# A gated linear recurrence followed by a SiLU block: 32x32 transposes of k and q that write their blocks side by side

## The chip, the cores and the metric

The kernel runs on one core of one Trainium2 chip. The metric is the device time of one execution in microseconds (us). Before the change the median of three runs is 561.26 us (560.49, 561.26 and 562.18).

## The reference

Two blocks follow each other. The first is a recurrence over 768 tokens for each of 4 batches and 8 heads of 48 dimensions; the second takes its output, laid out as 3072 tokens of 384 values, through two matrices with SiLU between them. All data are float32 on the chip.

```python
for t in range(S):                       # q, k, v, alpha: (4, 8, 768, 48)
    state = alpha[:, :, t, :, None] * state + np.einsum('bhd,bhe->bhde', k[:, :, t], v[:, :, t])
    y[:, :, t] = np.einsum('bhd,bhde->bhe', q[:, :, t], state)
x = y.transpose(0, 2, 1, 3).reshape(3072, 384)
h = x @ w_in                             # (384, 2048)
g = h * (1.0 / (1.0 + np.exp(-h)))
out = g @ w_out                          # (2048, 384)
```

## The kernel before

The recurrence is cut into 24 chunks of 128 tokens: 6 stretches of time for each of 4 batches (`NT = 24`; chunk n has stretch `n // 4` and batch `n % 4`). Within a chunk the products of alpha are taken by scans, so that the recurrence becomes ordinary matrix products: `kp` is k times a product of the alphas that follow, `p` (also called `qp`) is q times a product of the alphas up to it divided by a common factor, and the scores are `kp` against `qp`, masked so that no token sees a later one. A state of 48x48 for each head carries from chunk to chunk.

Heads are handled in pairs: in the tiles that the scans use, partition 64u + d holds dimension d of the heads with number 2g + u, and the free axis holds the four pairs g with 128 tokens each. The inputs come from memory with tokens, not dimensions, across the partitions, so they have to be transposed. The first 8 chunks (`n < NA`) do this on TensorE. The other 16 do it on VectorE, 32x32 elements at a time, and these are what the change is about.

For these 16 chunks `load` (L466) brings in `at`, `kt` and `qt` (alpha, k and q, four DMAs each). A partition holds four consecutive tokens of each head pair: token 4b + j lies in row b of a block of 32 rows, at place j, with its 48 dimensions side by side. `turned` (L694) transposes all of this in one VectorE instruction: for each pair g and each j it takes 32 rows by 32 dimensions and turns them into 32 dimensions by 32 values of b. These 32 values belong to tokens j, 4 + j, 8 + j and so on, so before the change they are written with a step of four elements, which puts the 128 tokens of a pair into their natural order.

Three tiles are made this way in each chunk:

- `al` from `at`, in `products` (L698). A scan over it (L722) gives `u`, and later another one (L752, in `quotient`) gives `p`. The scans need the tokens in order.
- `turn` from `kt`, in `products` (L730). It is multiplied by `u` into `kp`: L737 for the first two head pairs, L739 for the other two, whose halves of 64 tokens are written in exchanged order.
- `turn` from `qt`, in `quotient` (L742, transposed at L756). It is multiplied by `p` in place (L758).

After a transpose the tile that it has read is free, and the next chunk's load into it is issued at once. `turn` is one buffer, used in turn by the k tile, the q tile and `flip` (L760), which transposes `kp` once more (L768) and sends it through memory to turn it over for the state update.

Around this runs the SiLU block for tokens that are already through the recurrence. `enter` (L917) multiplies by `w_in` with a scheme that saves products at the price of sums on VectorE (L944, and sums of inputs and of weights at L582 to L587); `leave` (L1021) multiplies by `w_out` in a like manner (L1033, L1042, L1074 to L1085). Their pieces are dealt out over the steps by a plan of due times (`fill`, L1166), four slots a step. A step of a late chunk holds the scores of the chunk before, then `products` and `quotient` of its own, then the values and states of the chunk before. `audit` (L657) checks the inputs' magnitudes by reading them once more and reducing them on VectorE (L685).

TensorE's instructions of this part, the copies and scalings marked so, and VectorE's sums of inputs and of weights keep the order in which the program gives them; the others may be moved within their engine by a scheduler that goes by its own estimates of cost. All loads are issued from SP's queue, the stores up to the last group from GpSimd's.

Of the kernel before, what the change touches and what calls it, by code (L numbers as in the profile page):

```python
# [13 lines left out]
ALU = mybir.AluOpType  # L14
# [341 lines left out]
def quotients(  # L356
# [20 lines left out]
    dve, act, gps = nc.vector, nc.scalar, nc.gpsimd  # L377
# [25 lines left out]
    CH = C // 2  # L403
# [28 lines left out]
    def out_bank(i, n):  # L432
        return outs[i].tile([128, 512], F32, name="ps_o")[:, 0:n]

    def ps_attn(n=C):
        return ps_a.tile([128, 512], F32, name="ps_a").rearrange("p (j c) -> p j c", c=n)
# [29 lines left out]
    def load(n, names="akq"):  # L466
        if n == NT:
            return
        c = ctxs.setdefault(n, dict(zip(("ci", "b"), divmod(n, B))))
        b, rows = c["b"], slice(c["ci"] * C, c["ci"] * C + C)  # L470
        for name, src in (("a", alpha), ("k", k), ("q", q)):
            if name not in names:
                continue
            x = src[b, :, rows, :]
            if n < NA:
                c[name] = nat[name][n % NIN]
                nc.sync.dma_start(c[name][:, :, 0:D], x.transpose([1, 0, 2]))
                continue

            c[name] = late["quads"][name]
            for u in range(2):
                for i in range(2):
                    r = 64 * u + 32 * i
                    nc.sync.dma_start(
                        c[name][r : r + 32, 32 * (1 - i) :][:, 0 : 4 * NP * D].rearrange(
                            "p (g c) -> p g c", g=NP),
                        x[u::2].rearrange("h (b j) d -> b h (j d)", j=4))
# [48 lines left out]
    def turns(x, n):  # L538

        return x[(n + 1) % 2]  # L540
# [149 lines left out]
    def tokens(t):  # L690

        return t[:, 1 : NP * W + 1].rearrange("p (j c) -> p j c", c=W)[:, :, 0:C]

    def turned(x, to):  # L694
        x = x[:, 32:].rearrange("p (g j d) -> p g j d", j=4, d=D)
        dve.transpose(to.rearrange("p g (b j) -> p g j b", j=4), x[:, :, :, 0:32])

    def products(n):  # L698

        c = ctxs[n]  # L700
        sg = seg[0 if late else n % 2]
        ps = {}

        for name in ("a", "k", "q"):
            if n >= NA:
                if name == "a":
                    turned(c[name], tokens(sg))
                    load(n + 1, "a")
                continue
            if n < GB and name != "a":  # L710

                at = "kq".index(name)
                ps[name] = (bank(at) if n == 1 else out_bank(at, 512)).rearrange("p (j c) -> p j c", c=C)
            else:
                ps[name] = ps_attn()
            for j in range(NP):
                pe.transpose(ps[name][:, j, :], c[name][:, 2 * j : 2 * j + 2, :], ident)
            if name == "a":
                act.copy(tokens(sg), ps[name])  # L719
        end = NP * W  # L720
        u = upool.tile([128, end + 1], F32, name="u")
        dve.tensor_tensor_scan(u[:, end - 1 :: -1], sg[:, end:0:-1], one[:, end:0:-1],  # L722
                               0.0, ALU.mult, ALU.add)

        dve.tensor_single_scalar(least[:, n, :], u[:, 0:end:W], 2.0**-64, ALU.max)
        kp = c["kp"] = turns(kps, n) if n < NA else kps[0]
        ut = tokens(u)
        if n >= NA:
            ps["k"] = late["turn"].tile([128, NP, C], F32, name="turn")
            turned(c["k"], ps["k"])  # L730
            load(n + 1, "k")
        if n < NA:
            dve.tensor_tensor(kp, ps["k"], ut, ALU.mult)
            quotient(n, sg, ps["q"])
            return
        j = NP // 2
        dve.tensor_tensor(kp[:, 0:j], ps["k"][:, 0:j], ut[:, 0:j], ALU.mult)  # L737
        k, ut = [x[:, j:].rearrange("p j (e c) -> p j e c", e=2) for x in (ps["k"], ut)]
        dve.tensor_tensor(kp[:, j:].rearrange("p j (e c) -> p j e c", e=2)[:, :, ::-1], k, ut, ALU.mult)  # L739
        c["sg"] = sg  # L740

    def quotient(n, sg=None, q=None):  # L742

        c = ctxs[n]
        if sg is None:
            if n < NA:
                return
            sg = c.pop("sg")
        end, iv = NP * W, inv
        dve.reciprocal(iv[:, 0:end:W], least[:, n, :])  # L750
        p = turns(qps if n < NA else [qps[0], late["p"]], n)
        dve.tensor_tensor_scan(p[:, 0:end], sg[:, 0:end], iv[:, 0:end], 0.0, ALU.mult, ALU.add)  # L752
        qp = c["qp"] = tokens(p)
        if q is None:
            q = late["turn"].tile([128, NP, C], F32, name="turn")
            turned(c["q"], q)  # L756
            load(n + 1, "q")
        dve.tensor_tensor(qp, q, qp, ALU.mult)  # L758

    def flip(n):  # L760
# [133 lines left out]
    def bank(i, n=512):  # L894
        return banks[turn[i]].tile([128, 512], F32, name="ps_m")[:, 0:n]
# [289 lines left out]
    for step in range(STEPS):  # L1185
        if step == 1:
            load(NIN)
        stages = [[(scores, 1)], [(products, 0)], [(values, 1)], [(states, 1)]]
        if step == 1:

            stages = stages[1::-1] + stages[2:]
        elif step >= NA:
            stages = [[(land, 1), (scores, 1)], [(products, 0)], [(quotient, 0)],
                      [(values, 1), (states, 1), (flip, 0)]]
        for slot, group in enumerate(stages):
            for stage, lag in group:
                n = step - lag
                if not 0 <= n < NT:
                    continue
                stage(n)  # L1200
                if stage is values:
                    bridged = n + 1
                if stage is states and n + 1 + NIN < NA:
                    load(n + 1 + NIN)
                if stage is states and n + NV < NT:
                    load_v(n + NV)
            if step * SLOTS + slot == (NA + 1) * SLOTS - 1:
                x = decayed.rearrange("p (o i c) -> p o i c", o=2, c=C)
                for r, o in later:
                    gps.memset(x[r, o, :, 0:CH], 0.0)  # L1210
            fill(step, slot)
            if step * SLOTS + slot >= NA * SLOTS - 1 and conv_done[1] == NFT and not late:
                settle()
# [12 lines left out]
    for i, (x, op, bound, holds) in enumerate(checks):  # L1226
        e = ends[:, i : i + 1]
# [6 lines left out]
    ps = ps_attn()[0:1, 0, 0:1]  # L1234
# [64 lines left out]
```

## Time and profile before

The profiled execution has a span of 558.1 us; the median of the runs is 561.26 us, 3.2 us more, which lies around the span.

| what | value |
|---|---|
| span of the profiled execution | 558.1 us |
| median of three runs | 561.26 us |
| granted TensorE clock, mean of the core | 0.994 |
| L696 `al` transposes | 16 of 1134 ns |
| L722 scan to `u`, L752 scan to `p` | 24 of 1249 ns, 24 of 1246 ns |
| L944 products' sums from PSUM | 56 of 684 ns |
| L1033 sums | 72 of 708 ns |
| DMA, mean rate | 126 GB/s |

In the views that follow, PE is TensorE, PEld its loading of weights, DVE VectorE, ACT ScalarE and POOL GpSimd. A row of groups gives line, engine, operation, what is written and read, the shapes, the number of instructions, then after the bar their busy time in us and the mean of one in ns, and after the second bar the engine's idle time just before them with what ended it. A row of the timeline gives start and length in us, and in brackets the idle time before it and the instruction that ended that wait. A row of waits gives who waited for whom: us in total, how many times, and the longest. An instruction of VectorE that depends on the one before it starts after that one's end; one that doesn't can start a little before it.

### The profile page before, as it was taken

How to read it: one execution, taken by the hardware profiler on the slowest of the kernel's cores; microseconds unless marked ns; L12 is line 12 of the kernel's file. 1: busy time of each engine (PE TensorE's matmuls, PEld its weight loads, DVE VectorE, ACT ScalarE, POOL GpSimd, SP SyncE). 2: the span in 40 equal slices, each digit the busy share in tenths (PEclk: the TensorE clock that was granted, in tenths of full speed). 3: DMA queues.
4: the chain of work that ended last, by engine and by line, in shares of the span. 5: the costliest groups of instructions: out<-in, count | busy, mean ns of one | idle time of the engine just before them, and what ended most of it. 6: DMA issues, size and time to landing. Idle time of an engine off the chain costs nothing. (4 is left out here: it accounts for less than half of the span.)

```text
span 558.1 us, 12640 instructions
## 1 busy us (share of the span) xinstructions
PE 541.4 (97%) x5026; PEld 488.8 (88%) x5026; DVE 445.1 (80%) x801; ACT 208.4 (37%) x466; POOL 75.9 (14%) x146
## 2 busy tenths in 40 slices
PE   5999999999999999999999999999999999999996
PEld 3788887998899898899999999988998999998996
DVE  5887889974999799997998986998894775857531
ACT  3456643223333243353353353353263341432200
POOL 4100010221211211021021021021121000001000
PEclk9799999999999999999999999999999999999999
DMA  9999861164445525355445654717712122333101
GB/s 218 255 276 177 232 189 40 38 164 108 126 131 136 142 62 134 88 145 157 129 109 142 194 141 115 198 22 179 180 48 84 53 99 95 111 109 106 38 25 32
DMA packets 99220, 70.13 MB, mean 126 GB/s; under 512 B 56272, under 2 KB 88656, under 8 KB 99152
## 3 DMA queue, kind: packets, MB, share of 16 engines
q1 hardware_dynamic: 97232, 65.30, 44.6%
q0 software_dynamic: 1920, 3.93, 2.0%
q8 instruction: 41, 0.67, 0.5%
q14 instruction: 27, 0.22, 0.1%
HBM read 61.34 MB, written 7.86 MB: 124 GB/s over the span
## 5 line engine op out<-in xcount | busy, mean ns | idle before, releaser
L388 PE MATMUL ps_o<-w_out,g 128*128 128x192 f32 x768 | 134.7, 329 | 1.1 <-DVE o L1042 0.9
L388 PEld LDWEIGHTS ps_o<-w_out,g 128*128 128x128 f32 x768 | 125.4, 190 | 5.1 <-DVE o L1042 2.3
L388 PE MATMUL ps_m<-xt,w_in 128*128 128x256 f32 x480 | 113.6, 383 | 1.5 <-ACT xt L851 1.1
L388 PEld LDWEIGHTS ps_m<-xt,w_in 128*128 128x128 f32 x480 | 89.1, 190 | 14.4 <-ACT xt L851 1.6
L388 PE MATMUL ps_o<-wt,g 128*128 128x192 f32 x576 | 99.7, 326 | 0.0
L388 PEld LDWEIGHTS ps_o<-wt,g 128*128 128x128 f32 x576 | 95.1, 190 | 1.6 <-issue 0.2
L388 PE MATMUL ps_m<-xc,w_in 128*128 128x256 f32 x288 | 70.7, 382 | 0.0
L685 DVE TENSOR_REDUCE seen<-bits 128x1 f32<-128x384 int32 (+2 forms) x65 | 42.5, 689 | 24.0 <-DMA bits<-in_moe_w_out_dram 19.6
L388 PEld LDWEIGHTS ps_m<-xc,w_in 128*128 128x128 f32 x288 | 53.6, 190 | 7.0 <-DVE g L944 0.3
L941 ACT ACTIVATE g<-g 128x1024 f32<-128x1024 f32 x32 | 33.0, 1056 | 59.0 <-DVE g L944 59.0
L1033 DVE TENSOR_TENSOR g<-g 128x512 f32<-128x512 f32 x72 | 49.8, 708 | 6.1 <-PE ps_o L388 6.1
L1045 POOL DMA_DIRECT2D out_dram<-o x40 | 22.0, 550 | 223.2 <-DVE o L1042 127.6
L813 POOL TENSOR_SCALAR_AFFINE_SELECT g<-g 64x256 f32<-64x256 f32 x64 | 34.2, 534 | 124.8 <-ACT g L806 105.8
L388 PE MATMUL ps_m<-xc,wx 128*128 128x256 f32 x192 | 50.0, 383 | 1.0 <-DVE xc L586 1.0
L936 ACT COPY g<-ps_m 128x512 f32<-128x512 f32 x64 | 36.5, 588 | 36.5 <-PE ps_m L388 36.4
L388 PEld LDWEIGHTS ps_m<-xc,wx 128*128 128x128 f32 x192 | 35.2, 190 | 5.3 <-ACT u L1064 1.3
L944 DVE TENSOR_TENSOR g<-ps_m,g 128x512 f32<-128x512 f32 x56 | 37.0, 684 | 2.9 <-PE ps_m L388 2.7
L722 DVE TENSOR_TENSOR_SCAN u<-al,one 128x516 f32<-128x516 f32 x24 | 30.0, 1249 | 10.6 <-ACT al L719 10.3
L909 ACT ACTIVATE g<-ps_m 128x512 f32<-128x512 f32 x32 | 19.1, 596 | 42.8 <-PE ps_m L388 42.3
L936 ACT COPY part<-ps_m 128x512 f32<-128x512 f32 x32 | 18.9, 589 | 43.0 <-DVE g L944 21.3
L752 DVE TENSOR_TENSOR_SCAN p<-al,inv 128x516 f32<-128x516 f32 x24 | 29.9, 1246 | 1.0 <-PE ps_a L388 0.4
L388 PE MATMUL ps_a<-g,vn 128*32 128x128 f32 x768 | 27.5, 278 | 1.8 <-POOL g L801 1.7
(126 smaller groups left out, 611.4 us busy)
## 6 DMA issues: line engine op xcount, KB each, us to landing
bits<-in_moe_w_in_dram SPq DMA_DIRECT2D x24, 512.0 KB, 4.8
bits<-in_moe_w_out_dram SPq DMA_DIRECT2D x32, 384.0 KB, 3.1
at<-in_alpha_dram SPq DMA_DIRECT2D x64, 96.0 KB, 2.5
kt<-in_k_dram SPq DMA_DIRECT2D x64, 96.0 KB, 2.5
qt<-in_q_dram SPq DMA_DIRECT2D x64, 96.0 KB, 2.6
bits<-in_alpha_dram SPq DMA_DIRECT2D x9, 512.0 KB, 3.8
out_dram<-o POOLq DMA_DIRECT2D x40, 96.0 KB, 2.4
flips<-turn SPq DMA_DIRECT2D x12, 256.0 KB, 2.4
```

The lines of the kernel that those rows point to most:

```text
L388: in_order(nc.tensor.matmul(*args, **kw))
L685: dve.tensor_reduce(seen[kind][which][:, i : i + 1], x, axis=AX, op=op, apply_absolute_value=True))
L722: dve.tensor_tensor_scan(u[:, end - 1 :: -1], sg[:, end:0:-1], one[:, end:0:-1], 0.0, ALU.mult, ALU.add)
L752: dve.tensor_tensor_scan(p[:, 0:end], sg[:, 0:end], iv[:, 0:end], 0.0, ALU.mult, ALU.add)
L813: gps.affine_select(x, x, pattern=[[0, NP], [1, CH]], compare_op=ALU.is_ge, fill=0.0, base=0, channel_multiplier=-1)
L909: act.activation(gts[grp, h, pair][:, i : i + 2, q % 2, :], ps, AF.Silu)
L936: act.copy(to, ps)
L941: act.activation(x, x, AF.Silu)
L944: dve.tensor_tensor(to, a, b, op)
L1033: dve.tensor_tensor(cells(grp, h, pair, *to), cells(grp, h, pair, *x), cells(grp, h, pair, *y), ALU.subtract)
L1045: (gps if grp < NG - 1 else nc.sync).dma_start(out[r : r + C, c * HO : (c + 1) * HO], o)
```

## The change

`turned` no longer puts the step into every destination; its caller does. For alpha the caller passes the same destination as before. For k and q it passes `turn` with the blocks side by side: the 32 values of each (g, j) are written as one run, and the tokens of a pair then lie in the order j, b instead of b, j. The products that read `turn` name the tokens in their natural order (b outside, four values of j inside), so that within each group of four they step by 32 elements through `turn`, while their other operand and their result are contiguous. The exchanged halves of the last two head pairs, one instruction before (L739), are two instructions after the change[...]. Nothing else is changed.

```diff
     def turned(x, to):
         x = x[:, 32:].rearrange("p (g j d) -> p g j d", j=4, d=D)
-        dve.transpose(to.rearrange("p g (b j) -> p g j b", j=4), x[:, :, :, 0:32])
+        dve.transpose(to, x[:, :, :, 0:32])
...
-                    turned(c[name], tokens(sg))
+                    turned(c[name], tokens(sg).rearrange("p g (b j) -> p g j b", j=4))
...
-            turned(c["k"], ps["k"])
+            turned(c["k"], ps["k"].rearrange("p g (j b) -> p g j b", j=4))
...
-        dve.tensor_tensor(kp[:, 0:j], ps["k"][:, 0:j], ut[:, 0:j], ALU.mult)
-        k, ut = [x[:, j:].rearrange("p j (e c) -> p j e c", e=2) for x in (ps["k"], ut)]
-        dve.tensor_tensor(kp[:, j:].rearrange("p j (e c) -> p j e c", e=2)[:, :, ::-1], k, ut, ALU.mult)
+        kt = ps["k"].rearrange("p g (i b) -> p g b i", i=4)
+
+        def by_four(x):
+            return x.rearrange("p g (b i) -> p g b i", i=4)
+
+        dve.tensor_tensor(by_four(kp[:, 0:j]), kt[:, 0:j], by_four(ut[:, 0:j]), ALU.mult)
+        for e in range(2):
+            dve.tensor_tensor(by_four(kp[:, j:, CH * (1 - e) : CH * (2 - e)]),
+                              kt[:, j:, CH // 4 * e : CH // 4 * (e + 1)],
+                              by_four(ut[:, j:, CH * e : CH * e + CH]), ALU.mult)
...
-            turned(c["q"], q)
+            turned(c["q"], q.rearrange("p g (j b) -> p g j b", j=4))
             load(n + 1, "q")
+            q, qp = q.rearrange("p g (j b) -> p g b j", j=4), qp.rearrange("p g (b j) -> p g b j", j=4)
         dve.tensor_tensor(qp, q, qp, ALU.mult)
```

## The prediction

> **What bounds the kernel now.** I read the page's busy shares first, then the stages, then VectorE's groups by shape, and last the waits with the instructions around them.
>
> ```profile
> PE 541.4 (97%) x5026; PEld 488.8 (88%) x5026; DVE 445.1 (80%) x801; ACT 208.4 (37%) x466; POOL 75.9 (14%) x146
> 139.25:421.00 281.75, 278.89 (x2865) 254.63 (x2855) 259.14 (x452) 111.81 (x272) 44.62 (x81) 1.00 0.48 130
> 190.00:257.00 67.00, 65.65 (x660) 59.57 (x659) 65.61 (x122) 26.61 (x64) 9.08 (x17) 1.00 0.39 103
> ```
>
> Columns of the stage lines: stage, its length, busy us of PE, PEld, DVE, ACT, POOL. TensorE sets the time. VectorE is close behind it just where the change lies: from 139 to 421 us, where 15 of the 16 changed chunks run, it has 281.75 - 259.14 = 22.6 us idle, 1.5 us a chunk; from 190 to 257 us it has 1.4 us in all, and there TensorE idles too.
>
> ```profile
> L696 DVE STREAM_TRANSPOSE turn<-kt 128x512 f32<-128x512 f32 x16 | 18.2, 1136 | 0.0
> L696 DVE STREAM_TRANSPOSE turn<-qt 128x512 f32<-128x512 f32 x16 | 17.8, 1116 | 0.3
> L768 DVE STREAM_TRANSPOSE turn<-kp 128x512 f32<-128x512 f32 x12 | 8.5, 708 | 0.1
> L737 DVE TENSOR_TENSOR kp<-turn,u 128x256 f32<-128x256 f32 x16 | 7.2, 450 | 0.5
> L739 DVE TENSOR_TENSOR kp<-turn,u 128x256 f32<-128x256 f32 x16 | 7.2, 448 | 0.0
> L758 DVE TENSOR_TENSOR p<-turn,p 128x512 f32<-128x512 f32 x16 | 11.0, 687 | 0.2
> L685 DVE TENSOR_REDUCE seen<-bits 128x1 f32<-128x512 int32 x24 | 15.5, 681 | 4.4 <-DMA bits<-in_moe_w_in_dram 4.4
> ```
>
> All three transposes take 16 blocks of 32x32. L768 writes its blocks as runs, L696 with a step of 4 elements; L768 takes 0.41 to 0.43 us less. The last row reads every second element, at no visible cost.
>
> ```profile
> PE ps_m L388 <- DVE g L944: 1.3, 2, 0.9
> PE ps_m L388 <- DVE xc L586: 1.0, 1, 1.0
> PE ps_a L388 <- DVE p L758: 0.5, 1, 0.5
> ...
> 139.25 0.69 DVE L1019 TENSOR_TENSOR g<-g 128x512 f32<-128x512 f32 x1 [7.62 <-ACT g L909]
> 139.86 1.13 DVE L696 STREAM_TRANSPOSE turn<-kt 128x512 f32<-128x512 f32 x1
> 141.09 0.42 DVE L737 TENSOR_TENSOR kp<-turn,u 128x256 f32<-128x256 f32 x1
> 141.44 0.42 DVE L739 TENSOR_TENSOR kp<-turn,u 128x256 f32<-128x256 f32 x1
> 141.89 1.11 DVE L696 STREAM_TRANSPOSE turn<-qt 128x512 f32<-128x512 f32 x1
> 143.03 0.69 DVE L758 TENSOR_TENSOR p<-turn,p 128x512 f32<-128x512 f32 x1
> 143.87 0.90 PE L388 MATMUL ps_a<-p,kp 48*64 48x128 f32 x32 [0.48 <-DVE p L758]
> 219.37 1.13 PE L388 MATMUL ps_m<-xt,wx 128*128 128x256 f32 x4 [0.92 <-DVE g L944]
> 230.72 1.13 PE L388 MATMUL ps_m<-xt,w_in 128*128 128x256 f32 x4 [0.41 <-DVE g L944]
> 369.77 1.10 PE L388 MATMUL ps_m<-xc,wx 128*128 128x256 f32 x4 [1.02 <-DVE xc L586]
> ```
>
> So TensorE waits for VectorE four times in this stretch, 0.48 + 0.92 + 0.41 + 1.02 = 2.83 us in all. The first wait stands right behind one chunk's kt, kp, qt, p work. VectorE's timeline has no idle time of over 0.15 us from 139.25 to 182.2 us and from 188.4 to 254.6 us; before 188.4 it waits 2.49 us for ScalarE. In such a run whatever is added or saved is handed on to the next wait.
>
> [...] the 16-byte step of L696 costs 0.41 to 0.43 us in 512 elements, and the 8-byte step of L685 nothing. For a read with a step of 128 bytes no row exists. [...]
>
> **The change part by part.** For each of 16 chunks:
> - kt and qt transposes become runs like L768: 1.136 - 0.708 = 0.428 and 1.116 - 0.708 = 0.408, together -0.836 us. The at transpose stays.
> - The product for kp goes from two instructions to three. [...] +0.13 us.
> - The reads of turn with the step: call their extra r per 512 elements, once for q and once for k: +2r.
>
> Net a chunk: d = 2r - 0.70 us; break-even at r = 0.35.
>
> r is the unknown. [...] The nearest measured thing, the scattered write, gives 0.41. I take 0.45[...]. Then d = +0.20 us, and VectorE's busy time goes from 445.1 to about 448.3 us.
>
> The order of the instructions on TensorE, ScalarE, GpSimd and SP is unchanged. On VectorE it is the same but for the third kp instruction, up to the tenth of the 16 chunks (273 us), where the at transpose and its scan fall behind a few sums and products; after 350 us a few neighbours swap. These chunks' scores start 5 to 14 us after their p is ready, which hides it; I book 0, within 0.3 either way. ScalarE, idle 63%, and GpSimd, idle 86%, have nothing to do with turn.
>
> On the path, wait by wait, with r = 0.45 (DMAs are untouched):
> - 143.87: one whole chunk in front since VectorE was last idle: +0.20.
> - 219.37: in the run from 188.4 stand one q product alone (its transpose came before the idle time) and one whole chunk: 0.45 + 0.20 = +0.65.
> - 230.72: since then kt, kp and qt, but p only afterwards: -0.428 + 0.13 + 0.45 - 0.408 = -0.26, less than the 0.41 waited.
> - 369.77: a whole chunk, then kt and half of kp: 0.20 - 0.43 + 0.22 = 0.0.
>
> Sum +0.6 us. Scores that do not wait now have some slack by the timeline: 0.83 us in the next chunk (L758 ends at 159.24, they start at 160.07) and 1.10 us in the one after (175.19, 176.29); two chunks' lag beyond TensorE's own, 0.4 us, stays inside. The span is 558.1 us, the median of the runs 561.26; the 3.2 us around the span are not touched, so the sum goes on the median: **561.9 us**. With r from 0.3 to 0.6 the same four steps give -0.7 to +1.9: 560.5 to 563.1.
>
> **The rivals.**
> - *The strided read is free* (r = 0, d = -0.70). The waits shrink by 0.48, 0.70, 0.41 and 1.02 (each no more than it is, the third capped, the last saving 1.13): -2.6, 558.6 us. For it: a step of two elements is free.[...]
> - *The strided read is dearer, and VectorE's lag becomes TensorE's wait* (slower). Place: the runs without idle time; it decides from r about 0.6 (+1.9 us). At r = 1.07, d = 1.43, 15 x 1.43 = 21.5 of the 22.6 us idle are gone. First run: +1.43, then 1.43 - 0.83 = 0.60 and, with 1.10 - 0.83 = 0.27 of slack left, 1.43 - 0.27 = 1.16: 3.2. Second: 1.07 + 1.43 = 2.5, then +0.36 at 230.72 and about 1 after: 3.9. At 369.77, 1.43 - 0.43 + 0.54 = 1.5, and about 1 elsewhere: +9.6, 570.9 us. For it: no run of this kernel reads like this[...].[...]
> - *The transposes get no cheaper*, since their reads (32 of every 48 elements) cost the 1.12 us: d = 2 x 0.45 + 0.13 = 1.03. Then 1.03 + 0.20 + 0.76 in the first run, 1.48 + 0.58 in the second, 1.25 at 369.77: +5.3, 566.6 us. Against: L768 also reads runs of 32, with jumps between.
>
> **How the numbers follow.** A measurement here can tell about 0.3%, 1.7 us, from no change. Chances: forecast 0.53 (0.48 within 0.3%, 0.05 above), free read 0.15 (faster), dear read 0.25 and transposes no cheaper 0.07 (both slower). So faster 0.15, same 0.48, slower 0.37. The range 558.4 to 567.0 leaves out the dearest reads and little else.
>
> **What would show it.** L696's turn rows at about 0.71 us; the q product at 1.14 instead of 0.69; the kp products near 0.67 (128x256) and twice 0.40; VectorE busy near 448; TensorE's wait at 143.9 longer by 0.2, that at 219 by 0.6, that at 231 shorter. It is wrong if the q product stays at 0.69 (faster) or exceeds 1.3 us (slower), or if the transposes stay above 1 us.

## The result: 562.58 us after against 561.11 us before

In the shared runs the kernel before took 561.11 us (median of 20, 560.26 to 562.24) and the changed one 562.58 us (median of 20, 561.27 to 563.87). The ratio is 1.0025, 95% interval 1.0017 to 1.0033: +1.4 us, with an interval from 0.95 to 1.85. That is clear of zero, but of the size that the prediction called no change (0.3%, 1.7 us). The forecast was 561.9 us, +0.6.

The page's busy shares of the kernel after, then its row for the stage that the prediction showed as 139.25 to 421 us (columns: stage, length, busy us of PE, PEld, DVE, ACT and POOL; the stage starts 1.19 us earlier because this execution's first loads came sooner):

```profile
PE 540.5 (96%) x5026; PEld 487.5 (87%) x5026; DVE 445.4 (80%) x817; ACT 208.6 (37%) x466; POOL 76.4 (14%) x146
138.06:419.95 281.89, 278.84 (x2864) 254.58 (x2853) 259.08 (x467) 111.81 (x272) 44.82 (x81) 1.00 0.49 130
```

VectorE is busy for 445.4 us (445.1 before), and the stage has its old length, 281.89 us against 281.75. VectorE's groups of the changed lines after:

```profile
L696 DVE STREAM_TRANSPOSE turn<-qt 128x512 f32<-128x512 f32 x16 | 11.3, 706 | 0.3
L696 DVE STREAM_TRANSPOSE turn<-kt 128x512 f32<-128x512 f32 x16 | 11.2, 701 | 0.0
L742 DVE TENSOR_TENSOR kp<-turn,u 128x256 f32<-128x256 f32 x16 | 9.8, 611 | 0.5
L744 DVE TENSOR_TENSOR kp<-turn,u 128x128 f32<-128x128 f32 x32 | 10.8, 376 | 0.0
L766 DVE TENSOR_TENSOR p<-turn,p 128x512 f32<-128x512 f32 x16 | 17.0, 1061 | 0.2
```

The transposes fell by 0.435 and 0.410 us, 0.845 us a chunk. q's product rose from 687 to 1061 ns, so the extra r of the step is 0.374 us for 512 elements. k's product rose from 450 + 448 = 898 ns to 611 + 2 x 376 = 1363 ns, +0.465: r again, and the third instruction. How this divides was not measured: with q's r it leaves 0.09 us for the instruction, with the rise of the 128x256 product (161 ns for half of the elements) 0.14. The sum is d = -0.006 us a chunk: what the transposes save, the products take.

This sum counts the durations of the records. Where the next instruction of VectorE doesn't depend on a transpose, it starts before the transpose has ended: on average 0.21 us (k) and 0.16 us (q) before it with scattered blocks, in 13 of the 32 cases, and 0.06 and 0.07 us with blocks side by side. There the transpose's saving, from one start to the next, is only 0.31 and 0.33 us, while q's product costs 0.37 us more by this measure too. So d is about zero in a chain of dependent instructions, where each next one starts 0.03 to 0.11 us after the transpose's end (16 cases), as in front of the wait at 143.87, and above zero elsewhere.

The four waits of TensorE that the prediction went through, in the timeline of the kernel after:

```profile
142.68 0.90 PE L388 MATMUL ps_a<-p,kp 48*64 48x128 f32 x32 [0.46 <-DVE p L766]
218.55 1.13 PE L388 MATMUL ps_m<-xt,wx 128*128 128x256 f32 x4 [0.92 <-DVE g L952]
229.58 1.13 PE L388 MATMUL ps_m<-xt,w_in 128*128 128x256 f32 x4 [0.38 <-DVE g L952]
368.74 1.10 PE L388 MATMUL ps_m<-xc,wx 128*128 128x256 f32 x4 [1.02 <-DVE xc L586]
```

They are 0.46, 0.92, 0.38 and 1.02 us, before 0.48, 0.92, 0.41 and 1.02. So the 1.4 us have to come from somewhere else. In this pair of profiles TensorE ends 0.8 us later (554.30 against 553.50) and the span 2.0 us later (560.14 against 558.10). The 0.8 us up to TensorE's end turned out to be mostly an accident of the pair; the 1.2 us behind it did not.

### The profile page after: what moved, and what is told of

It is laid out like the page before. It is cut to its first block, busy times and chain, and to the rows that moved or that the text cites. A ratio compares the mean times of both kernels' runs of the same rounds, so it can differ in the third digit from the quotient of the medians.

```text
span 560.1 us, 12657 instructions
## 1 busy us (share of the span) xinstructions
PE 540.5 (96%) x5026; PEld 487.5 (87%) x5026; DVE 445.4 (80%) x817; ACT 208.6 (37%) x466; POOL 76.4 (14%) x146
## 5 line engine op out<-in xcount | busy, mean ns | idle before, releaser
L685 DVE TENSOR_REDUCE seen<-bits 128x1 f32<-128x384 int32 (+2 forms) x65 | 42.5, 687 | 27.0 <-DMA bits<-in_moe_w_out_dram 22.7
```

Source lines behind the costliest of these rows:

```text
L685: dve.tensor_reduce(seen[kind][which][:, i : i + 1], x, axis=AX, op=op, apply_absolute_value=True))
```

## Experiments

Ratios below are to the kernel before, run on the same chip beside each experiment. The absolute times differ from one set of runs to the next (the kernel before had 559.11, 559.21 and 561.28 us in the three sets), so only ratios are compared across sets.

### The same two kernels again, and both without the audit of the weights

In the first profiles VectorE's stretch from 450 to 520 us, where `audit` reads w_out and reduces it, was 1.6 us longer after the change. Two theories: the audit's loads now meet VectorE at a worse moment (tail), or VectorE's new durations cost time between 120 and 420 us (middle). Two runs repeat the kernels; two leave out the check of the weights' magnitudes, which is part of the computation's guard and not of its output:

```diff
     def audit():
+        wide = False
...
-    if wide:
+    if len(seen) > 1:
         checks += [(seen[1][0]
```

> The kernel before, unchanged, as a measure of how far two builds of the same program differ. If the 1.5 us between before and after are no more than the luck of one load of a program: differs from before by about 1 us too. If they belong to the change: within 0.3 us of before, and the 16 loads of the weight audits between 450 and 520 us land in 3.0 us again.

> The changed kernel once more. Belongs to the change: again 1.2 to 1.8 us over before. Luck: anywhere between -1 and +1.5 us.

> The kernel before without the audits of w_in and w_out (their loads, reductions and checks are left out). VectorE no longer waits for these loads from 340 to 520 us. Both theories: faster than before by 1 to 5 us, as TensorE's waits at 478 and 515 us go. It is the partner of the next kernel.

> The changed kernel without the audits of w_in and w_out. Theory tail (the 1.5 us are VectorE's waits for these loads after 450 us, where the code is the same): within 0.5 us of the kernel before without these audits. Theory middle (the changed products delay TensorE between 139 and 421 us): 1 to 1.8 us over it, as before against after.

Measured: the kernel before again 1.0004 [0.9992, 1.0016]; the kernel after again 1.0037 [1.0021, 1.0052]; without the audit, before's version 0.9992 [0.9981, 1.0004] and after's 0.9988 [0.9977, 0.9998]. Leaving the audit out was expected to save before's version 1 to 5 us, and the median fell by 0.3: TensorE's last product ends 1.7 us earlier (551.03 against 552.77 in the kernel before again), but the end behind it is 1.35 us longer, for the reason found below. Without the audit the two kernels are level. Yet the tail theory was not the reason: in the repeated profiles TensorE ends at the same time, 552.77 us (before) and 552.76 us (after), while the spans are 557.37 and 558.72 us. The whole difference, 1.35 us, lies behind TensorE's last product. These are the records of SyncE's queue there (start, end in us), which the timeline leaves out because they are waits and branches; the two middle columns of each row are operation and line:

```
before again                                   after again
553.25 553.58 DMA_DIRECT2D    L1045  store     553.24 553.57 DMA_DIRECT2D    L1053  store
553.63 553.71 COMPARE_BRANCH  L1267            553.62 553.69 COMPARE_BRANCH  L1275
554.16 554.18 EVENT_SEMAPHORE L1267            (nothing)
554.26 554.27 EVENT_SEMAPHORE L1267
554.34 554.36 EVENT_SEMAPHORE L1267
554.43 554.44 EVENT_SEMAPHORE L1267
555.45        the store lands                  555.72        the store lands
555.47 555.48 EVENT_SEMAPHORE L1267            556.48 556.49 EVENT_SEMAPHORE L1275
...                                            ...
557.37        end of the span                  558.72        end of the span
```

After the last store SyncE jumps over the fallback `general`, which these inputs don't need, and then goes through a fixed list of waits that ends the program. Before, it goes on 0.45 us after the jump and stands waiting for the store when this lands. After the change it goes on 2.79 us after the jump, 0.76 us after the landing, and the list starts late: from the landing to the end of the span 3.00 us instead of 1.92. That is 1.08 us; the other 0.27 us is the store's own landing, which comes back below. In the first pair of profiles the same two distances are 1.93 and 2.88 us.

VectorE's jump at the same end takes 2.81 to 3.16 us in every kernel here, before and after. Behind the last store the instruction queue (q14 of the page) moves three packets of 8,192 bytes in the kernel before and four in the kernel after. Both kernels without the audit have SyncE's late jump too (2.77 and 2.70 us, four packets), which fits their being level. What was left to find is why SyncE's jump in the kernel before is quick.

In the compiled program of SyncE, the kernel after has one instruction more: a load of q at about 377 us waits for two things now, in place of one, since a few neighbours on VectorE changed places. So three places of the jump move by one: its hint, the branch itself (602 to 603) and its target (896 to 897). 896 is 7 x 128. That a target at a multiple of 128 makes the jump quick was the author's guess, shown by no trace before; it made the target the first suspect.

### Moving the target alone

A drain added to SyncE in the skipped fallback moves before's target from 896 to 900; three loads of the fallback moved to another queue bring after's from 897 back to 896.

```diff
+    for _ in range(1):
+        nc.sync.drain()
```
```diff
-        nc.sync.dma_start(c["v"], v[b, :, rows, :].transpose([1, 0, 2]))
+        (act if n < 3 else nc.sync).dma_start(c["v"], v[b, :, rows, :].transpose([1, 0, 2]))
```

> The kernel before, with a drain of SyncE added in the fallback that these inputs skip. Nothing that runs is changed; of SyncE's program the branch and all before it stay where they are, and the branch's target moves from instruction 896 = 7x128 to 900. Theory end (the step of after comes from SyncE's jump over the fallback[...]): SyncE's next instruction 2.5 to 2.8 us after the branch's end (0.45 in the kernel before), from the last store's landing to the end of the span 2.9 to 3.3 us (1.93), ratio to the kernel before 1.0015 to 1.0030. Theory middle (the step comes from VectorE's work or the order of the loads): 0.45 us, 1.93 us, ratio 1.000 within 0.0008. If the store's landing itself goes from 1.86 to about 2.14 us here too, that part is the program's layout as well.

> The kernel after, with three loads of the skipped fallback moved from SyncE's queue to ScalarE's, so that SyncE's branch target is instruction 896 again (897 in after); nothing that runs is changed. Theory end: SyncE's next instruction 0.45 us after the branch's end, from the last store's landing to the end of the span 1.9 us, ratio to the kernel before 0.9990 to 1.0010. Theory middle: ratio 1.0020 to 1.0040, as after's. Should the store's landing stay at 2.14 us, the ratio keeps about 0.0005 above one.

Measured: with the drain 0.9995 [0.9986, 1.0004], the jump still 0.45 us; with the three loads 1.0014 [1.0002, 1.0026], the jump still 2.65 us, 3.16 us from the landing to the end. The guess about the target fell with both. That the late jump makes the step was not touched by this; the place that decides had to be that of the hint or of the branch.

### Moving the hint and the branch

In SyncE's program the hint stands between the first and the second store of the last group. So the first of these stores, moved to GpSimd's queue, shifts hint and branch; the second shifts only the branch; and the last store of the group before, moved from GpSimd's queue to SyncE's, shifts both the other way. Three guesses are told apart by this: that the hint's place decides (hint), that the branch must not stand at 603 or later (branch), or that only a branch at 602 is quick (chance place).

```diff
-            (gps if grp < NG - 1 else nc.sync).dma_start(
+            (gps if (grp, h, m, c) <= (NG - 1, 0, 0, 0) else nc.sync).dma_start(
```
```diff
-            (gps if grp < NG - 1 else nc.sync).dma_start(
+            (gps if grp < NG - 1 or (h, m, c) == (0, 0, 1) else nc.sync).dma_start(
```
```diff
-            (gps if grp < NG - 1 else nc.sync).dma_start(
+            (gps if grp < NG - 1 and (grp, h, m, c) != (NG - 2, 1, 1, 0) else nc.sync).dma_start(
```

> The kernel after, with the first store of the last group on GpSimd's queue, where the groups before have theirs. It stands before SyncE's branch hint (on at about 524 us, 34 us ahead of the end), so hint and branch both come one instruction or two earlier in SyncE's program: hint 593 as in the kernel before (594 in after), branch 601 (602 before, 603 after). Theory hint (where the hint stands decides[...]): SyncE goes on 0.45 us after its branch, 1.9 us from the last store's landing to the end, ratio to the kernel before 0.999 to 1.001. Theory branch (the branch must not stand at 603 or later): the same. Theory chance place[...]: 2.7 us, 2.9 to 3.1 us, ratio 1.001 to 1.003. Theory middle (the step lies in the recurrence): ratio 1.001 to 1.003 with 0.45 us or with 2.7.

> The kernel after, with the second store of the last group (about 530 us) on GpSimd's queue. It stands behind the hint, so the hint stays at 594 and the branch comes to 601. Theory hint: SyncE goes on 2.7 us after its branch, ratio to the kernel before 1.001 to 1.003. Theory branch: 0.45 us, ratio 0.999 to 1.001. Theory chance place: 2.7 us, 1.001 to 1.003.

> The kernel before, with the last store of the group before the last on SyncE's queue (GpSimd's in before), ahead of the hint: hint at 594, branch at 604. All three places for the jump give 2.7 us from the branch to SyncE's next instruction, 2.9 to 3.1 us from the last store's landing to the end, and a ratio to the kernel before of 1.0012 to 1.0025; theory middle gives 0.999 to 1.0005 with the jump's 0.45 us.

All kernels of the study together, with the places in SyncE's compiled program, and from each one's trace the time from the end of the branch to SyncE's next instruction, from the end of the last store's issue to its landing, and from there to the end of the span:

| kernel | hint, branch, target | branch to next, us | store to landing, us | landing to end, us | ratio |
|---|---|---|---|---|---|
| before | 593, 602, 896 | 0.45 | 1.86 | 1.93 | 1 |
| before again | 593, 602, 896 | 0.45 | 1.87 | 1.92 | 1.0004 |
| before, drain | 593, 602, 900 | 0.45 | 1.91 | 1.92 | 0.9995 |
| after, first store | 593, 601, 895 | 0.45 | 2.15 | 2.00 | 1.0014 |
| after | 594, 603, 897 | 2.66 | 2.14 | 2.88 | 1.0025 |
| after again | 594, 603, 897 | 2.79 | 2.15 | 3.00 | 1.0037 |
| after, three loads | 594, 603, 896 | 2.65 | 1.86 | 3.16 | 1.0014 |
| after, second store | 594, 601, 895 | 2.55 | 1.87 | 3.04 | 1.0021 |
| before, store more | 594, 604, 897 | 2.84 | 2.13 | 3.07 | 1.0030 |
| runs only (below) | 593, 602, 896 | 0.45 | 2.19 | 1.92 | 0.9938 |
| step reads only (below) | 594, 603, 896 | 2.80 | 2.19 | 2.98 | 1.0083 |
| step 33 (below) | 594, 603, 897 | 2.60 | 2.00 | 2.97 | 1.0028 |
| before, no audit | 540, 557, 851 | 2.77 | 1.85 | 3.28 | 0.9992 |
| after, no audit | 540, 557, 851 | 2.70 | 2.13 | 2.93 | 0.9988 |

The two kernels with the branch at 601 settle it between hint and branch: with the hint at 593 the jump takes 0.45 us, with the hint at 594 it takes 2.55. Every kernel with the hint at 593 is quick and every other one is not, wherever branch and target stand. The packets say the same: behind the last store the instruction queue moves three in each of the five quick executions and four in each of the nine late ones. And with the hint at 593 SyncE comes to it 0.04 us after the instruction in front, with the hint at 594 after 0.34 us, in all seven. Whether this pause and the late jump have a common cause was not tried. The two kernels without the audit, at 540, have no such pause (0.06 us), but their hint comes 92 us ahead of the jump in place of 26; what makes theirs late is open.

The times follow less sharply than the traces. The kernel before with its hint moved to 594 is slower, 1.0030 [1.0013, 1.0046], though no part of its recurrence was touched: the moved store and the late jump alone can make such a step. The point is above the 1.0012 to 1.0025 that was expected; in its trace the landing came 0.27 us later as well. The kernel after with its hint moved back to 593 came to 1.0014 [1.0001, 1.0026], where 0.999 to 1.001 was expected, and after with its hint at 594 and the same branch to 1.0021 [1.0010, 1.0033]; these two intervals overlap, so it is the traces that tell them apart. Of the 0.8 us that stay at 593, with an interval from 0.06 to 1.5, the recurrence explains 0.2 (below), and the trace has 0.36 us more than before behind TensorE's last product: 0.29 in the store's landing and 0.07 in one more wait of the list behind it. The rest is within the interval.

The store's landing takes 1.85 to 1.91 us in six of these profiles and 2.00 to 2.19 in the other eight. It goes neither with SyncE's jump (after with three loads has 1.86 us and a late jump, the runs only 2.19 and a quick one) nor with the change (before with the store more has 2.13). It does go with VectorE's jump at the end: that takes 2.81 to 2.88 us in the six, 2.98 to 3.16 in the eight. So the store is not slow alone; what the two have in common was not shown. The two programs with two profiles repeat their landing (1.86 and 1.87 us before, 2.14 and 2.15 after), which speaks for a property of the program; what sets it is open.

### The two halves of the change, each alone

Side-by-side transposes with the contiguous products of the kernel before, and the scattered transposes with the products of the kernel after. Both leave out the order of the tokens in k and q.

```diff
-        dve.transpose(to.rearrange("p g (b j) -> p g j b", j=4), x[:, :, :, 0:32])
+        dve.transpose(to, x[:, :, :, 0:32])
...
-            turned(c["k"], ps["k"])
+            turned(c["k"], ps["k"].rearrange("p g (j b) -> p g j b", j=4))
...
-            turned(c["q"], q)
+            turned(c["q"], q.rearrange("p g (j b) -> p g j b", j=4))
```

For the second, the kernel after with its two callers passing `(b j)` in place of `(j b)`, so that `turned` scatters again, and the three loads of the fallback.

> Transposes of k and q (and the last of a) as in after, side by side, with the products of the kernel before, which read contiguously: the four tokens' order is left out, so k and q of a chunk's tokens stand in another order. VectorE loses 0.845 us a chunk, 13.5 us of 445.1, and SyncE's branch target stays at 896. Theory path (VectorE's products before the four waits of TensorE, 3.48 us in all a profile, set part of the time): 1 to 3 us faster, ratio 0.9945 to 0.9982. Theory slack (all four waits end by other things): within 0.4 us, ratio 0.9993 to 1.0007.

> Transposes as in the kernel before, scattered, with after's products that read in steps of 32 and in three instructions for k: the tokens' order is left out as well. Three loads of the skipped fallback are on ScalarE's queue, so that the branch's target stays 896. VectorE gains 0.84 us a chunk, 13.4 us of 445.1. Theory path: 1.5 to 4 us slower, ratio 1.0025 to 1.0070. Theory slack: ratio within 0.0007 of one, plus 0.0005 if the store's landing lengthens. Either way q's product is expected at 1.06 us and k's three at 0.61, 0.38 and 0.38.

Measured: runs only 0.9938 [0.9922, 0.9955], 3.5 us faster; step reads only 1.0083 [1.0067, 1.0099], 4.6 us slower. Of the latter, about 1.1 us are the late jump (2.80 us in its trace: the target at 896 didn't make it quick, so the expectation's premise failed there), so the two halves are nearly mirror images, -3.5 and +3.5. Both lie beyond the far end of what was expected. So VectorE's work in front of the waits does set the time, and the slack theory is out. TensorE's rows at the first three waits with the runs only, and below them with the step reads only:

```profile
142.31 0.90 PE L388 MATMUL ps_a<-p,kp 48*64 48x128 f32 x32
216.86 1.13 PE L388 MATMUL ps_m<-xt,wx 128*128 128x256 f32 x4
227.48 1.13 PE L388 MATMUL ps_m<-xt,w_in 128*128 128x256 f32 x4
138.20:417.00 278.80, 278.69 (x2867) 254.90 (x2857) 248.38 (x452) 112.36 (x273) 45.04 (x81) 1.00 0.48 131
```

```profile
144.01 0.73 PE L388 MATMUL ps_a<-p,kp 48*64 48x128 f32 x23 [1.23 <-DVE p L766]
177.03 0.90 PE L388 MATMUL ps_a<-p,kp 48*64 48x128 f32 x32 [0.36 <-DVE p L766]
221.31 1.13 PE L388 MATMUL ps_m<-xt,wx 128*128 128x256 f32 x4 [1.75 <-DVE g L952]
```

With 0.845 us a chunk less in VectorE's records the three waits are gone from the timeline, and TensorE's modelled busy time fills the stage, 278.69 of 278.80 us. With 0.84 us more the waits grow by about that much (0.48 to 1.23, 0.92 to 1.75), and a new one stands at 177 us. VectorE's busy time itself falls to 434.8 us and rises to 457.5, by 10.3 and 12.4 us and not by the 13.5 and 13.4 that were expected from durations; it counts records that overlap only once. The change does both at once, and ends where it began.

### Where the recurrence still loses a little

The order of TensorE's products is the same in all these kernels, so each product's start can be compared with its start in the kernel before. The distance, taken as the median over 4 us around a time of the kernel before, less its value at 120 us, in us:

| kernel | 150 | 200 | 205 | 226 | 233 | 240 | 300 | 400 |
|---|---|---|---|---|---|---|---|---|
| before again | -0.01 | -0.01 | -0.01 | -0.01 | -0.01 | -0.01 | -0.01 | -0.01 |
| before, drain | 0.00 | 0.00 | 0.00 | 0.00 | 0.01 | 0.01 | 0.00 | 0.00 |
| after | -0.03 | -0.03 | 0.35 | 0.35 | 0.03 | 0.21 | 0.15 | 0.15 |
| after again | -0.04 | -0.04 | 0.36 | 0.36 | 0.05 | 0.25 | 0.19 | 0.20 |
| after, first store | -0.05 | -0.05 | 0.33 | 0.33 | 0.01 | 0.19 | 0.13 | 0.14 |

This stretch repeats to a few hundredths of a us, while the time up to 120 us (loads) and after 420 us (the audit's loads) differs by up to 2 us between two executions of the same kernel. From 400 to 520 us TensorE falls back by 1.4 to 2.1 us in the first profile after the change and in all four of the third set, the kernel before with a store more among them; in the others that keep the audit it moves by -0.4 to +0.3 us. That is the accident of the first pair. The change costs 0.14 to 0.20 us here: +0.38 at 203.8 us, -0.32 at 229, +0.18 at 236.6, -0.06 at 285. The jump at 203.8 starts on VectorE at 188 us. The timelines of VectorE, ScalarE and TensorE before:

```profile
188.43 0.69 DVE L1019 TENSOR_TENSOR g<-g 128x512 f32<-128x512 f32 x1 [2.49 <-ACT g L909]
189.03 0.68 DVE L758 TENSOR_TENSOR p<-turn,p 128x512 f32<-128x512 f32 x1
203.04 0.58 ACT L936 COPY part<-ps_m 128x512 f32<-128x512 f32 x1 [3.90 <-DVE g L944]
203.81 1.89 PE L388 MATMUL ps_m<-xc,w_in 128*128 128x256 f32 x8
```

The same instructions after:

```profile
187.23 0.69 DVE L1027 TENSOR_TENSOR g<-g 128x512 f32<-128x512 f32 x1 [2.88 <-ACT g L917]
187.84 1.08 DVE L766 TENSOR_TENSOR p<-turn,p 128x512 f32<-128x512 f32 x1
202.25 0.58 ACT L944 COPY part<-ps_m 128x512 f32<-128x512 f32 x1 [4.30 <-DVE g L952]
202.88 1.59 PEld L388 LDWEIGHTS ps_m<-xc,w_in 128*128 128x128 f32 x8 [0.40 <-ACT part L944]
202.88 1.99 PE L388 MATMUL ps_m<-xc,w_in 128*128 128x256 f32 x8
```

The transposes of this chunk stand ahead of a wait for ScalarE. What they save only lengthens that wait, 2.49 to 2.88 us; what the product adds comes behind it, and VectorE has no gap from there to 202 us. ScalarE's copy waits 0.40 us longer for VectorE's sum, and TensorE for ScalarE's copy out of `ps_m`; the wait stands in the row of the weight loads (PEld). The next chunk's cheaper transposes give most of it back at 229 us, again at a wait that the rows of products hardly show. The weight load there, before and after, and ScalarE's work in front of the scores at 236.6 us, before and after:

```profile
229.18 0.73 PEld L388 LDWEIGHTS ps_m<-xc,w_in 128*128 128x128 f32 x4 [0.32 <-DVE g L944]
228.04 0.75 PEld L388 LDWEIGHTS ps_m<-xc,w_in 128*128 128x128 f32 x4
233.96 2.02 ACT L941 ACTIVATE g<-g 128x1024 f32<-128x1024 f32 x2 [1.60 <-DVE g L944]
235.87 0.45 ACT L851 COPY xt<-ps_a 128x384 f32<-128x384 f32 x1
233.21 2.00 ACT L949 ACTIVATE g<-g 128x1024 f32<-128x1024 f32 x2 [2.00 <-DVE g L952]
235.12 0.46 ACT L859 COPY xt<-ps_a 128x384 f32<-128x384 f32 x1
```

The step at 236.6 us is of the same kind as the one at 203.8. That chunk's product of q stands behind the wait at 229 us, its transpose in front of it; ScalarE's activations wait 0.40 us longer for VectorE's sum, the copy of `xt` behind them ends 0.26 us before the scores' start in the kernel before and only 0.05 us before it after the change, so that there the scores wait for ScalarE.

In the two kernels without the audit the same steps stand at 203.8, 229 and 236.6 us (+0.38, -0.31, +0.18), and from 380 us on the one after the change is 0.09 us ahead: there the recurrence loses nothing in the end.

### Another step

The blocks of `turn` put 33 elements apart in place of 32:

```diff
-            q = late["turn"].tile([128, NP, C], F32, name="turn")
-            turned(c["q"], q.rearrange("p g (j b) -> p g j b", j=4))
+            q = late["turn"].tile([128, NP, 132], F32, name="turn")
+            turned(c["q"], q.rearrange("p g (j b) -> p g j b", j=4)[:, :, :, 0:32])
```

and k likewise, with the products reading the same view.

> The kernel after with the blocks of k's and q's turned tiles 33 elements apart in place of 32, so that the products read in steps of 33. If any step over a row of elements costs the same: q's product 1.06 us, k's three 0.61 and 2 x 0.38, time within 0.5 us of after's. If it is the step of 32 (128 bytes) that collides: q's product 0.69 to 0.8 us, k's 0.42 to 0.5 and 0.27 to 0.33, 0.3 us or more a chunk for each, and 2 to 3 us faster than after. The transposes' writes stay in runs of 32 and should keep their 0.70 us.

Measured: 1.0028 [1.0009, 1.0048], as the kernel after. Its groups:

```profile
L766 DVE TENSOR_TENSOR p<-turn,p 128x512 f32<-128x512 f32 x16 | 17.0, 1061 | 0.2
L744 DVE TENSOR_TENSOR kp<-turn,u 128x128 f32<-128x128 f32 x32 | 10.8, 375 | 0.0
L742 DVE TENSOR_TENSOR kp<-turn,u 128x256 f32<-128x256 f32 x16 | 9.8, 610 | 0.5
```

The durations are those of the step of 32 to within 1 ns. So it is not that the distance of 128 bytes collides with something: a step of 132 bytes costs the same. Other steps were not tried.

No version of the study that keeps the tokens' order and the guard beats the kernel before. The runs without step reads would, but would need tokens j, 32 + j, ... brought to one partition by the loads, in pieces of one token's 192 bytes in place of four tokens' 768; that was not tried.

## Why the prediction came out right, point by point

- *The transposes become runs like L768.* Right: 0.701 and 0.706 us where 0.708 was taken. The rival that they get no cheaper is out.
- *The extra r of a read with the step.* Taken 0.45 us, an estimate of the author's that no row before showed, as was the 1.07 at which the dear read was priced; measured 0.374, between free and the 0.41 to 0.43 of the scattered write. Both rivals on r are out: it is neither 0 nor above 0.6. The term was a fifth too large; the prediction's own break-even of 0.35 was nearly met.
- *The third instruction for kp.* Taken +0.13 us, also an estimate of the author's: no row before shows a product of 128x128. 0.09 to 0.14 of the measured +0.465 can be its share.
- *Net a chunk.* Taken +0.20 us, measured -0.006 by the durations; busy time of VectorE 445.4 us, not 448.3.
- *Wait by wait.* The rule, that a cost is handed on from one wait to the next, was right; the price of r was too high, and the list of waits was too short. At 143.87 a whole chunk stands in front: with the measured d this gives 0, and the wait went from 0.48 to 0.46. At 219.37 one product without its transpose and one chunk: r + d = 0.37, and TensorE was 0.35 us later there; but it lost this at 203.8 already, through ScalarE's copy, so the wait at 219 kept its 0.92. At 230.72, -0.26: 0.32 us were won at 229, on a weight load, and the wait at 230.72 itself only went from 0.41 to 0.38. At 369.77, 0.0: its wait is 1.02 us as before. The sum was +0.6; the profiles show 0.14 to 0.20 up to 400 us, part of it at 236.6, where nothing was booked. The list came from the rows of products alone. VectorE's delay also reaches TensorE through ScalarE, which the prediction said has nothing to do with `turn`, and in the weight loads, whose longest wait for VectorE before the change, at 219.37, is 1.32 us where the products' row has 0.92.
- *What was not priced.* "DMAs are untouched" and "the 3.2 us around the span are not touched" were taken to mean that the end is as before. (Around the span lie only 1.7 to 1.9 us in every execution whose span is known; the rest of the 3.2 is that the profiled execution was quicker than the median.) The order on VectorE was looked at for its waits, not for what it does to another engine's instruction count: SyncE got one more wait at 377 us, its hint moved by one place, and its jump at the end became late, for 0.95 to 1.1 us in the traces. The kernel before with a moved hint, 1.0030, shows that such a step comes without any change to the recurrence.

So the main ground held: what the transposes save, the products take, and little of either reaches TensorE. The nearness of the number is in part luck: the recurrence was overpriced by some 0.4 us, and the end of the program, which had no term in the sum, brought about 1.0. Together with 0.2 that is 1.2 of the 1.4 us measured. The store's later landing, some 0.28 us in both pairs of profiles, would fill the rest, but that it belongs to the change is not shown; without it the remainder is within the interval (0.95 to 1.85 us).

## What to carry to other kernels

Here a transpose that scatters and a product that gathers cost nearly the same for each element (0.41 to 0.44 and 0.37 us for 512), so moving the step from one to the other gave nothing by itself; only the removal of both did, 3.5 us. When a saving and a cost stand on two sides of a wait, as at 188 us, the saving is lost in the wait and the cost is not. Waits of TensorE have to be looked for in its weight loads too. And before an effect of a microsecond is looked for in the loop, compare where the last product ends with where the span ends: here a change of VectorE's order moved SyncE's hint by one place, and its jump at the end of the program went from 0.45 to 2.66 us.

## What the runs showed of the hardware

- VectorE's product with one fp32 operand read with a step of 32 or of 33 elements takes 0.374 us more for 512 elements, 0.73 ns for each (k's of 256 elements 0.16 us more); a transpose that writes with a step of 4 elements takes 0.41 to 0.44 us more, of which 0.31 to 0.33 are left where the next instruction doesn't depend on it. In the reductions of L685 that read with a step of two elements nothing was seen: before the change they take 548 ns for 384 elements and 681 for 512, and the ones without a step 1209 for 1024, so 1.04 ns for each further element up to 512 and 1.03 beyond.
- SyncE's taken jump at the end of the program takes 0.45 us in some kernels, with three packets of the instruction queue behind the last store, and 2.55 to 2.84 us in the others, with four. The place of the hint in the program, at instruction 593 or 594, decided between the two; moving the target or the branch alone decided nothing. Without the audit, at 540, the jump is late too.
- Within an execution, the landing of the last store and VectorE's jump at the end are slow or quick together: 1.85 to 1.91 us with 2.81 to 2.88, and 2.00 to 2.19 with 2.98 to 3.16.
